# Plain fp32 products for batch 0's v and u, and a gate product in seven blocks for batches 1 to 7

## The chip, the cores and the metric

The program runs on one core of a Trainium2 chip. The metric is the time of one execution on the device, in microseconds (us). The core has TensorE (PE; its weight loads are PEld), VectorE (DVE), ScalarE (ACT), GpSimd (POOL) and SyncE (SP), which issues all DMAs here. Every engine works its own instructions off in order and waits for others by semaphores.

## The reference, cut to what matters

Eight batches. An attention over 8 heads, 576 positions and 64 columns (a pooled one over groups of 4 positions plus a local one over a band of 7) gives x; a gated MLP follows.

```
x = attention(q, k, v)                 # per batch 576 x 512
h = gelu(x @ w_in)                     # 512 -> 1024
u, v = h[..., :512], h[..., 512:]
v_n = (v - mean(v)) / sqrt(var(v) + 1e-6) * g_ln
v_s = einsum('ts,bsd->btd', w_sg, v_n) + b_sg[None, :, None]   # the gate product, 576 x 576
out = x + (u * v_s) @ w_out
```

## The kernel before, in words

Everything is kept turned: x, u and the gated product lie with the 512 columns on partitions (4 blocks of 128) and the 576 positions along the row, v with positions on partitions (4 blocks of 128 and one of 64).

`attention(b, p)` makes one pair of heads, 32 pairs in all, numbered g. It loads q, k and v (`lq`, `lk`, `lv`, `lw`), sums q, k and v over groups of four (`qs`, `ks`, `vs`), multiplies scores (`S`, the local ones, and `Y`, the pooled ones; from pair 4 on `YS` for both), takes maxima, exponentials and sums (`mx`, `my`, `ia`, `ib`, `ea`, `eb`, `ec`, `re`, `rc`), divides (`np`, `nq`), turns the probabilities on TensorE (`T`, `U`, `t`), copies them out of PSUM (`pa` to `pe`), multiplies with v (`D`) and writes x (`oe`, `od`, `xa`, `xb`). Then x is split into a high part in the rounded fp32 form that TensorE takes in one pass, and the rest (`xh`, `xl`, `xc`). These attention products are plain fp32 matmuls of 64 x 64 pieces, four of which run beside each other in the array.

`mlp(b)` makes three large products out of such splits; each is high x high, low x high and high x low: `v` (five blocks of 512 columns, in batch 0 in four steps each, `vk` and `v`), `u` (eight blocks of 288 columns), `s` (the gate product, eight blocks) and `o` (the output product). v goes through gelu (`vg`), mean and variance (`vb`), the root (`vp`), normalising (`vn`) and a split (`vh`, `vl`); u through gelu (`ua`); `sa` multiplies s by g_ln and adds b_sg on DVE, `sm` multiplies that with u. In batches 1 to 7 the output product is already made of seven block products per half instead of eight (`small_tasks`): sums of the gated blocks (`ga` to `gd`), their splits (`gh`, `gl`), products with combined weights (`zs`, `zh`, `zl`) and adds out of PSUM into x (`oa`). The result is stored by `os`.

The weights come as 64 bit words, are made fp32 by `wu`, `wq`, `wb` and `wt` and split by `wh` and `wl` (w_in as y0 to y3 for v and z0 to z3 for u, w_out as r0 to r3). The gate weights are fp32 and are split by `whq` and `wlq`.

What sets the order of the work is one list written out by hand, `ORDER`: each entry names a task and, behind a slash, its engine (without one, the first that the task names). `place` walks through it, gives each task its buffers (8 PSUM banks, 10 and 38 SBUF buffers) and the instructions are issued in that order, so every engine meets its share in it. A `dma` also waits for the sixth one before it. Ahead of `S0` stand 28 and ahead of `S3` 20 warming matmuls of zeros.

Lines that the rows below name: L244 is the copy helper, L481 `qs` and `ks`, L498 and L499 the two sums of `vs` on POOL, L514 and L535 the matmuls of `S` and `Y`, L613 `nq`, L693 part of `D`, L801 the matmuls of `v`, L896 those of `u`, `s` and batch 0's `o`, L887 `vl`, L943 `sa`, L924 `ua`, L1019 the seven block products of `o`, L1026 `oa`. L574, L596 and L817 are exponentials and gelus.

## Time and profile before

| | us |
|---|---|
| time, median of 3 runs (565.48 to 566.45) | 566.14 |
| the profiled execution, first to last instruction (its span) | 563.4 |
| PE busy | 547.7 (97%) |
| DVE busy | 445.5 (79%) |
| ACT busy | 392.7 (70%) |
| POOL busy | 331.9 (59%) |

For the profiled execution only its span is given; the time of the runs also holds what lies around the span, 2.7 us by the median. Busy time is the union of an engine's instructions. Matmuls overlap each other, so a mean of 295 ns for one does not say how far apart two start; the chain of work, which lists stretches of one line with their number, does. "<-" in a row of groups stands between what is written and what is read, and behind the bar stand the busy time, the mean ns of one, and the idle time of the engine just before them with what ended it. A window row has the length, then for each engine the busy us and in brackets its instructions, then the granted clock of TensorE, the share of the DMA engines and GB/s.

### The profile page before, as it was taken

Reading aid. Unit: us, or ns where it says so; the run is one execution under the profiler, and the core shown is the slowest. Engines: PE = TensorE matmul, PEld = TensorE weight load, DVE = VectorE, ACT = ScalarE, POOL = GpSimd, SP = SyncE. Lnnn points to the kernel's source line nnn. Section 1 sums busy time; section 2 is a strip of 40 time slices with the busy share of each in tenths; the row PEclk is TensorE's granted clock in tenths of the full one; section 3 lists DMA queues with packets and bytes.
Section 4 is the critical chain, followed back from the end, with each engine's and each line's share of the span. In section 5 each row is a group of like instructions: output and inputs, shape, how many; then the busy total and the mean of one; then the engine's idle time right before and its main releaser. Section 6 shows DMA issues by size and latency. Waiting matters only on the chain.

```text
span 563.4 us, 17546 instructions
## 1 busy us (share of the span) xinstructions
PE 547.7 (97%) x6948; PEld 511.2 (91%) x6948; DVE 445.5 (79%) x939; ACT 392.7 (70%) x1320; POOL 331.9 (59%) x447
## 2 busy tenths in 40 slices
PE   6888999999999999999999999999999999999997
PEld 4777899889998899989999899988999899999997
DVE  7998899977798887897869777886668786656565
ACT  2898899899876699177976976657956894525221
POOL 6895975856557665537764574528454573556222
PEclk8899999999999999999999999999999999999999
DMA  8879635310643144303441162403233224200004
GB/s 283 273 227 341 203 93 172 95 57 23 181 126 103 34 163 121 100 2 107 153 157 46 46 186 85 136 1 103 92 109 119 66 78 129 71 1 1 0 1 169
DMA packets 31041, 62.73 MB, mean 111 GB/s; under 512 B 3696, under 2 KB 4720, under 8 KB 30960
## 3 DMA queue, kind: packets, MB, share of 16 engines
q1 hardware_dynamic: 30960, 61.62, 34.3%
q8 instruction: 55, 0.90, 0.7%
q14 instruction: 26, 0.21, 0.1%
HBM read 52.17 MB, written 9.44 MB: 109 GB/s over the span
## 4 chain that ended last, share of the span: by engine, by line
PE 76%; ACT 6%; DVE 5%; POOL 4%; issue 2%; DMA 0%; DVEq 0%; ACTq 0%; POOLq 0%
PE ps L896 36%; PE ps L801 14%; PE ps L1019 12%; PE ps L677 3%; PE ps L693 2%; PE ps L616 2%; PE ps L625 2%; PE ps L535 2%; PE ps L514 2%; ACT X L574 2%; ACT R L244 1%; DVE R L990 1%; POOL pairs L498 1%; ACT pd L596 1%; POOL wsg_l L441 0%
## 5 line engine op out<-in xcount | busy, mean ns | idle before, releaser
L896 PE MATMUL ps<-wsg_h,R 128*128 128x288 f32 x576 | 122.5, 300 | 0.2 <-DVE R L887 0.2
L896 PE MATMUL ps<-X,weight_z 128*128 128x288 f32 x512 | 109.5, 297 | 0.3 <-ACT R L924 0.3
L801 PE MATMUL ps<-weight_y,X 128*128 128x512 f32 x320 | 98.3, 400 | 0.1
L574 ACT ACTIVATE X<-X,nb 128x64 f32<-128x64 f32 x280 | 93.5, 339 | 5.1 <-DVE nb L553 4.7
L896 PEld LDWEIGHTS ps<-wsg_h,R 128*128 128x128 f32 x576 | 93.9, 188 | 1.3 <-DVE R L887 0.4
L896 PE MATMUL ps<-wsg_l,R 128*128 128x288 f32 x320 | 92.6, 295 | 0.0
L896 PEld LDWEIGHTS ps<-X,weight_z 128*128 128x128 f32 x512 | 84.2, 188 | 1.2 <-ACT R L924 0.6
L896 PE MATMUL ps<-R,weight_z 128*128 128x288 f32 x256 | 75.4, 295 | 0.0
L801 PEld LDWEIGHTS ps<-weight_y,X 128*128 128x128 f32 x320 | 57.6, 188 | 11.9 <-POOL X L244 0.3
L1026 DVE TENSOR_TENSOR R<-ps,R 128x288 f32<-128x288 f32 x98 | 42.1, 448 | 25.2 <-PE ps L1019 24.9
L896 PEld LDWEIGHTS ps<-wsg_l,R 128*128 128x128 f32 x320 | 60.3, 189 | 0.0
L244 ACT COPY R<-ps 128x116 f32<-128x116 f32 (+3 forms) x80 | 27.2, 381 | 40.9 <-DVE R L244 11.9
L574 ACT ACTIVATION_READ_ACCUMULATOR X<-X,nb 128x1 f32 x280 | 53.3, 190 | 0.0
L1019 PE MATMUL ps<-R,weight_r 128*128 128x288 f32 x336 | 51.0, 298 | 0.3 <-DVE R L700 0.3
L244 ACT CAST R<-R 128x576 fp32r<-128x576 f32 (+2 forms) x61 | 39.1, 647 | 17.4 <-POOL R L990 10.5
L801 PE MATMUL ps<-weight_y,R 128*128 128x512 f32 x128 | 50.4, 394 | 0.0
L498 POOL TENSOR_TENSOR pairs<-R 112x256 f32<-112x256 f32 x56 | 45.0, 804 | 6.1 <-DMA R<-in_v_dram 6.0
L896 PEld LDWEIGHTS ps<-R,weight_z 128*128 128x128 f32 x256 | 48.2, 188 | 0.3
L943 DVE SCALAR_TENSOR_TENSOR vs<-ps,g_sb,b_sb 128x288 f32<-128x288 f32 x64 | 32.3, 512 | 20.1 <-PE ps L896 16.9
L1019 PEld LDWEIGHTS ps<-R,weight_r 128*128 128x128 f32 x336 | 46.6, 188 | 1.4 <-issue 0.5
L1002 POOL TENSOR_TENSOR R<-R,R 128x576 fp32r<-128x576 f32 x21 | 32.1, 1534 | 23.4 <-ACT R L244 9.8
L949 POOL TENSOR_TENSOR R<-R,vs 128x288 f32<-128x288 f32 x27 | 24.5, 909 | 35.4 <-DVE vs L943 29.4
(148 smaller groups left out, 1363.7 us busy)
## 6 DMA issues: line engine op xcount, KB each, us to landing
R<-in_v_dram SPq DMA_DIRECT2D x56, 224.0 KB, 3.5
X<-in_vw_dram SPq DMA_DIRECT2D x32, 320.0 KB, 4.4
R<-in_kT_dram SPq DMA_DIRECT2D x32, 293.0 KB, 3.9
R<-in_qT_dram SPq DMA_DIRECT2D x32, 293.0 KB, 3.8
out_dram<-R SPq DMA_DIRECT2D x28, 288.0 KB, 3.5
weight_z<-in_w_in_dram SPq DMA_DIRECT2D x4, 512.0 KB, 5.8
weight_y<-in_w_in_dram SPq DMA_DIRECT2D x4, 512.0 KB, 6.0
weight_r<-in_w_out_dram SPq DMA_DIRECT2D x4, 512.0 KB, 5.8
```

What stands on the lines that cost most here:

```text
L244: (nc.scalar.copy if e == "A" else ENG[e].tensor_copy)(**kw)
L498: ENG[e].tensor_tensor(out=pairs, in0=v[:, 0:2], in1=v[:, 2:4], op=ALU.add)
L514: nc.tensor.matmul(out=sp[i][os, c * KB:(c + 1) * KB], lhsT=q[hs, t * QB:t * QB + KB], rhs=k[hs, t * QB:t * QB + KB], start=not early, sto ...
L574: nc.scalar.activation(out=st["ms"][:, t, :], in_=src, func=AF.Exp, bias=st["nb"][:, t:t + 1], scale=scale, accum_out=sums[par][:, t:t + 1])
L677: nc.tensor.matmul(out=out, lhsT=lhsT, rhs=pdt[ks, probs, h * QC:(h + 1) * QC], start=first, stop=last)
L801: nc.tensor.matmul(out=acc, lhsT=r32(l), rhs=r32(weights[f"y{k}"][:, 0, w]), start=(i == 0 and ks[0] == 0), stop=(i == len(ops) - 1 and ks ...
L896: nc.tensor.matmul(out=acc[:, 0:HALF], lhsT=r32(l), rhs=r32(r), start=(first and n == 0), stop=(last and n == len(ops) - 1))
L943: nc.vector.scalar_tensor_tensor(out=vsb[i], in0=at["ps", "m", b, "s", i][:, 0:HALF], scalar=g_sb[:, i // 2:i // 2 + 1], in1=b_sb[:, half( ...
L949: ENG[e].tensor_tensor(out=gate(i), in0=gate(i), in1=vsb[i], op=ALU.mult)
L1002: ENG[e].tensor_tensor(out=r32(gl[m]), in0=us[raws[m]], in1=gh[m], op=ALU.subtract)
L1019: nc.tensor.matmul(out=bank(j, c), lhsT=r32(l), rhs=r32(r), start=first and i == 0, stop=i == len(ops) - 1, skip_group_check=not first)
L1026: nc.vector.tensor_tensor(out=x, in0=bank(j, c), in1=x, op=ALU.add)
```

## The change

Batch 0's v and u are made of plain fp32 matmuls with the whole weights and the whole x: 20 and 32 of them instead of 56 and 96, no split of x in batch 0, and the splits of w_in are first read by batch 1.

In batches 1 to 7 the first 512 of the 576 positions of the gate product are cut into two halves each way and made of seven block products per half of the columns and positions instead of eight: sums of normalised v blocks (`fa`, `fb`, `fd`, in place `fc`), their splits (`fh`, `fl`), combined gate weights made once (`ta`, `th`, `tl`), seven products for each of two column blocks, copies out of PSUM scaled by g_ln (`sx`) and joins (`sy`), and the gating (`sa`). The remaining 64 positions are added to four of the seven. The bias enters through these 64 positions' free rows, as b_sg / g_ln (`gr`, `gt`, `gs`, `br`, `bd`, `bs`, `be`; `vc` keeps a copy of the last block of v). The combined weights are written over parts of the old ones, after batch 0's last `s`.

`vs` can also run on DVE, as a reduction. The list `ORDER` is new throughout: other places, other engines. The diff, cut:

```diff
@@ ORDER @@
-wz3 wuz3 lk0 ks0/P wqz3/V wbz3 wy0 wqy0/V wby0 lq0 lk2 lk1 wtz3 whz3/A wlz3/P S0 lq1 qs0/V Y0 mx0 ia0 lq3 my0 ks1/P
-wuy0 qs1/P ib0 ea0 small wty0 S1 mx1 ks2/V lq2 qs2/P ia1 es0 ny0/A ec0 re0/A ib1 ea1 Y1 lk3 my1 rc0 S2 mx2 why0/A ia2
...
+lk0 ks0 lq0 S0 qs0 Y0 mx0 wz3 wqz3 lq1 wy0 my0 lk1 lk2 wbz3 ia0 ib0 qs1/P ks1/P ny0 wqy0 lq2 qs2/P ks2/P ea0 wby0 ec0
+wuz3 S1 mx1 lq3 es0 re0 lk3 Y1 my1 ny1 ec1 lv0 S2 mx2 ks3/P S3 rc0 np0 ia1 ib1 ea1 wuy0 wz0 ia2 ib2 T0 ea2 nq0 lq4 es1
...
@@ SMALL_S, and what is prepared once @@
-EARLY_S, EARLY_D, WIDE, SMALL_O = 4, 4, 4, 1
+EARLY_S, EARLY_D, WIDE, SMALL_O, SMALL_S = 4, 4, 4, 1, 1
...
+    def guard(out, g):
+        nc.vector.tensor_scalar(out=out, in0=g, scalar1=TINY, scalar2=2.0 * TINY, op0=ALU.is_lt, op1=ALU.mult)
+        nc.vector.scalar_tensor_tensor(out=out, in0=g, scalar=-TINY, in1=out, op0=ALU.is_gt, op1=ALU.mult)
+        nc.vector.tensor_tensor(out=g, in0=g, in1=out, op=ALU.add)
...
+    def g_turn(e):
+        raw, tmp = at["R", "w", "g"][up, 0:DM], buf("R", "w", "g2")[up, 0:DM]
+        guard(tmp, raw)
+        nc.vector.reciprocal(out=raw, in_=raw)
...
+    def b_rows_of(dst, raw):
+        nc.vector.tensor_copy(out=r32(dst), in_=raw)
+        nc.vector.tensor_tensor(out=raw, in0=raw, in1=dst, op=ALU.subtract)
+        nc.vector.tensor_scalar(out=r32(dst), in0=dst, scalar1=row_sb[up, 1:2], scalar2=None, op0=ALU.mult)
+        nc.vector.scalar_tensor_tensor(out=r32(dst), in0=raw, scalar=row_sb[up, 0:1], in1=dst, op0=ALU.mult, op1=ALU.add)
...
+    def t_sum(n):
+        def emit(e):
+            buf("R", "tr", n)
+            for i in range(2):
+                a, c = {1: lambda: (t_raw(i, False), t_raw(i, True)), 2: lambda: (t_raw(2 + i, False), t_part(1, i)),
+                        3: lambda: (t_raw(2 + i, False), t_raw(i, False)), 4: lambda: (t_raw(2 + i, True), t_part(2, i))}[n]()
+                ENG[e].tensor_tensor(out=t_part(n, i), in0=a, in1=c, op=ALU.subtract)
+        return emit
...
+    for n, raws, before in ((1, (0, 1), []), (2, (2, 3), ["ta1"]), (3, (0, 1, 2, 3), []), (4, (2, 3), ["ta2"])):
+        add(f"ta{n}", {"P": 1.5, "V": 0.8}, t_sum(n), [f"tq{i}" for i in raws] + before, takes=[("R", "tr", n)],
+            gives=[("R", "tq", i) for i in raws] + [("R", "tr", n - 1)] * len(before))
+        add(f"th{n}", {"A": 0.58, "V": 0.4}, t_high(n), [f"ta{n}"] + ([f"s{SMALL_S - 1}.{i}" for i in range(2 * KT)] if n == 1 else [f"sm{SMALL_S - 1}.{i}" for i in range(2 * KT)] if n == 3 else []))
+        add(f"tl{n}", {"P": 1.3, "V": 0.66}, t_low(n), [f"th{n}"], gives=[("R", "tr", n)])
@@ attention @@
+                if e == "V":
+                    nc.vector.tensor_reduce(out=vd[:, i], in_=v.rearrange("p f d -> p d f"), axis=AX.X, op=ALU.add)
+                    continue
-            add(N("vs"), {"P": 2.7}, vsum, [N("lv"), N("D", 2)], gives=[("R", "v4", g, 0), ("R", "v4", g, 1)])
+            add(N("vs"), {"P": 2.7, "V": 1.3}, vsum, [N("lv"), N("D", 2)], gives=[("R", "v4", g, 0), ("R", "v4", g, 1)])
+        if b == 0:
+            return
         add(N("xh"), {"A": 0.64, "V": 0.4}, x_high, [N("xa"), N("xb")], takes=[("X", "xh", g)])
@@ mlp: v and u of batch 0 @@
+                if first:
+                    for k in ks:
+                        l = sb[k]["x"][:, s * P:min(S, (s + 1) * P)]
+                        nc.tensor.matmul(out=acc[0:LEFT] if last else acc, lhsT=l, rhs=unsplit(f"y{k}"), start=k == 0, stop=k == KT - 1)
+                    return
...
+                if first:
+                    acc = buf("ps", "m", b, "u", i)[:, 0:HALF]
+                    for k in range(KT):
+                        l = block(unsplit(f"z{k // 2 * 2 + d}"))[:, k % 2, ds]
+                        nc.tensor.matmul(out=acc, lhsT=l, rhs=sb[k]["x"][:, cs], start=k == 0, stop=k == KT - 1)
+                    return
...
@@ mlp: the seven block products of batches 1 to 7 @@
+        def f_sum(n):
+            def emit(e):
+                buf("R", "f", b, n)
+                for i in range(2):
+                    near, far = vact[i][0], vact[2 + i][0]
+                    a, c, op = {1: lambda: (near[:, DM // 2:], far[:, DM // 2:], ALU.add),
+                                2: lambda: (f_tile(1)[:, i], near[:, 0:DM // 2], ALU.subtract),
+                                4: lambda: (far[:, 0:DM // 2], f_tile(2)[:, i], ALU.subtract)}[n]()
+                    ENG[e].tensor_tensor(out=f_tile(n)[:, i], in0=a, in1=c, op=op)
...
+        def f_self(i):
+            def emit(e):
+                v = vact[i][0]
+                ENG[e].tensor_tensor(out=v[:, DM // 2:], in0=v[:, 0:DM // 2], in1=v[:, DM // 2:], op=ALU.subtract)
...
+        def s_mm_s(j, n):
+            c, first_in = {1: "b", 2: "a", 5: "e"}.get(n) or {3: "e"}.get(n, "b"), n in (1, 2, 5)
+
+            def emit(e):
+                if first_in:
+                    buf("ps", "m", b, "s", j, c)
+                ops = []
+                for i in range(2):
+                    ops += [(s_left(n, i, x, j), s_right(n, i, y)) for x, y in ((0, 0), (1, 0), (0, 1))]
+                if n in (2, 3, 4, 7):
+                    ds = slice((j + (2 if n in (4, 7) else 0)) * P, (j + (3 if n in (4, 7) else 1)) * P)
+                    cs = slice(0, HALF) if n == 2 else slice(HALF, S)
+                    for l, c0 in ((vhat[NS - 1][0], 0), (last_sb, 1)):
+                        ops.append((l[:, ds], wsd[c0] if n == 4 else (wsg_h, wsg_l)[c0][:, NS - 1, cs]))
+                for i, (l, r) in enumerate(ops):
+                    nc.tensor.matmul(out=s_bank(j, c), lhsT=r32(l), rhs=r32(r), start=first_in and i == 0,
+                                     stop=i == len(ops) - 1, skip_group_check=not first_in)
+            return emit
...
+                    buf("R", "t", b, j, k // 2)
+                src, g = s_bank(j, "bbe"[k]), g_sb[:, d:d + 1]
+                if e == "A":
+                    nc.scalar.activation(out=s_part(j, k), in_=src, func=AF.Copy, scale=g)
+                else:
...
+            def emit(e):
+                nc.vector.scalar_tensor_tensor(out=s_part(j, k), in0=s_bank(j, "aeb"[k]), scalar=g_sb[:, d:d + 1], in1=s_part(j, k),
+                                               op0=ALU.mult, op1=ALU.add)
+            return emit
...
+            def emit(e):
+                if (r, t) == (1, 0):
+                    nc.vector.scalar_tensor_tensor(out=gate(i), in0=s_bank(j, "b"), scalar=g_sb[:, d:d + 1], in1=gate(i),
+                                                   op0=ALU.mult, op1=ALU.mult)
+                else:
+                    ENG[e].tensor_tensor(out=gate(i), in0=gate(i), in1=s_part(j, r + t), op=ALU.mult)
+            return emit
...
+        if small_s:
+            for n, need, used in ((1, [N("vn", i) for i in range(4)], (0, 1, 2, 3)), (2, [f"fa{b}"], (0, 1)), (4, [f"fb{b}"], (2, 3))):
+                gives = [("R", "v", b, i) for i in used] + ([("R", "f", b, {2: 1, 4: 2}[n])] if n > 1 else [])
+                add(f"f{'abcd'[n - 1]}{b}", {"P": 1.5, "V": 0.7}, f_sum(n), need, takes=[("R", "f", b, n)], gives=gives)
+                add(N("fh", n), {"A": 0.58, "V": 0.4}, f_high(n), [f"f{'abcd'[n - 1]}{b}"], takes=[("R", "fh", b, n)])
+                add(N("fl", n), {"P": 1.3, "V": 0.66}, f_low(n), [N("fh", n)], takes=[("R", "fl", b, n)], gives=[("R", "f", b, n)])
+            for i in range(2):
+                add(N("fc", i), {"P": 0.75, "V": 0.35}, f_self(i), [f"fa{b}"])
         for s in range(NS):
...
+            fac = {1: ["vl", 0, 1], 2: ["vl", 2, 3], 3: ["fl", 4], 4: ["vl", 2, 3], 5: ["fl", 1], 6: ["fl", 2], 7: ["vl", 0, 1]}
...
+                prod(1, "b", opens_bank=True)
+                add(X_(0), copied, s_copy(j, 0), [S_(1)] + (["sg"] if b == SMALL_S else []), takes=[t0])
+                prod(2, "a", opens_bank=True)
+                add(Y_(0), joined, s_join(j, 0), [S_(2), X_(0)], gives=[key("a")])
+                prod(6, "b", [X_(0)])
+                add(X_(1), copied, s_copy(j, 1), [S_(6), X_(0)])
+                prod(5, "e", opens_bank=True)
+                add(X_(2), copied, s_copy(j, 2), [S_(5)], takes=[t1])
+                prod(3, "e", [X_(2)])
+                add(Y_(1), joined, s_join(j, 1), [S_(3), X_(1)], gives=[key("e")])
+                prod(7, "b", [X_(1)])
+                add(Y_(2), joined, s_join(j, 2), [S_(7), X_(2)])
+                prod(4, "b", [Y_(2)])
+                for r, t, need, gives in ((0, 0, Y_(0), [t0]), (0, 1, Y_(1), [t0]), (1, 1, Y_(2), [t1]), (1, 0, S_(4), [key("b")])):
+                    i = 2 * (j + 2 * r) + t
+                    add(N("sa", i), {"V": 0.51} if gives[0][0] == "ps" else {"P": 0.83, "V": 0.46}, s_gate_s(i), [need, N("ua", i)], gives=gives)
         if small_o:
             small_tasks()
             return
...
```

## Rows read from the trace of the kernel before

**Rows 1.** The page's first part: busy time of each engine.
```profile
PE 547.7 (97%) x6948; PEld 511.2 (91%) x6948; DVE 445.5 (79%) x939; ACT 392.7 (70%) x1320; POOL 331.9 (59%) x447
```

**Rows 2.** Windows: stretch, length, PE, PEld, DVE, ACT, POOL busy, clock, DMA, GB/s.
```profile
0.00:60.00 60.00, 49.02 (x985) 40.34 (x989) 51.48 (x120) 43.76 (x146) 45.31 (x59) 0.94 0.87 279
60.00:88.00 28.00, 27.72 (x423) 25.80 (x414) 25.84 (x59) 26.39 (x83) 20.55 (x31) 1.00 0.47 160
88.00:173.20 85.20, 85.18 (x1178) 80.64 (x1176) 71.27 (x145) 74.30 (x263) 55.73 (x72) 1.00 0.32 96
173.20:540.00 366.80, 365.57 (x4234) 344.40 (x4228) 281.15 (x588) 244.52 (x822) 204.59 (x283) 1.00 0.27 84
```

**Rows 3.** Waits of TensorE, whole span: line, releaser, total us, times, longest.
```profile
PE ps L514 <- DMA R<-in_qT_dram: 2.3, 1, 2.3
PE ps L693 <- issue: 2.2, 1, 2.2
PE ps L535 <- DVE qd L481: 2.1, 2, 1.4
PE ps L625 <- POOL pd L613: 1.7, 1, 1.7
...
PE ps L535 <- ACT R L244: 0.7, 1, 0.7
```

**Rows 4.** The chain of waits: start us, us, what and how many.
```profile
114.26 2.78 PE ps L801 x12
126.22 12.73 PE ps L896 x96
...
547.55 12.70 PE ps L1019 x96
560.27 0.46 DVE R L1026
```

**Rows 5.** Groups by shape, TensorE: split products, then the pooled scores.
```profile
L896 PE MATMUL ps<-wsg_l,R 128*128 128x288 f32 x320 | 92.6, 295 | 0.0
...
L801 PE MATMUL ps<-weight_y,R 128*128 128x512 f32 x128 | 50.4, 394 | 0.0
...
L535 PE MATMUL ps<-kd,qd 64*64 64x144 f32 x256 | 16.5, 303 | 2.9 <-DVE qd L481 2.1 <-ACT R L244 0.7
...
L535 PE MATMUL ps<-kd,qd 64*64 64x48 f32 x128 | 11.1, 221 | 0.4 <-issue 0.4
```

**Rows 6.** Groups: weight loads of the gate product.
```profile
L896 PEld LDWEIGHTS ps<-wsg_l,R 128*128 128x128 f32 x320 | 60.3, 189 | 0.0
```

**Rows 7.** Groups: operations of DVE and POOL that the new ones resemble.
```profile
L498 POOL TENSOR_TENSOR pairs<-R 112x256 f32<-112x256 f32 x56 | 45.0, 804 | 6.1 <-DMA R<-in_v_dram 6.0
L1026 DVE TENSOR_TENSOR R<-ps,R 128x288 f32<-128x288 f32 x98 | 42.1, 448 | 25.2 <-PE ps L1019 24.9
L943 DVE SCALAR_TENSOR_TENSOR vs<-ps,g_sb,b_sb 128x288 f32<-128x288 f32 x64 | 32.3, 512 | 20.1 <-PE ps L896 16.9 <-issue 2.3 <-POOL R L949 0.5
L499 POOL TENSOR_TENSOR vd<-pairs 112x128 f32<-112x128 f32 x56 | 28.8, 514 | 4.4
L887 POOL TENSOR_TENSOR R<-R,R 128x512 fp32r<-128x512 f32 (+1 forms) x17 | 22.0, 1299 | 16.5 <-ACT R L244 5.4 <-DVE R L244 5.1 <-ACT R L924 4.1
L887 DVE TENSOR_TENSOR R<-R,R 128x512 fp32r<-128x512 f32 (+1 forms) x23 | 17.5, 767 | 4.2 <-ACT R L244 2.1 <-POOL rs L854 1.8
L481 DVE TENSOR_REDUCE qd<-R 128x144 f32<-128x576 f32 x23 | 17.1, 742 | 1.0 <-DMA R<-in_qT_dram 1.0
```

**Rows 8.** Groups: ACT's table loads, the first and the last of six lines.
```profile
L924 ACT ACT_TABLE_LOAD x13 | 16.7, 1283 | 0.4
...
L362 ACT ACT_TABLE_LOAD x1 | 1.3, 1283 | 0.7 <-PEq L1210 0.7
```

**Rows 9.** Groups: the seven block products of the output.
```profile
L1019 PE MATMUL ps<-R,weight_r 128*128 128x288 f32 x336 | 51.0, 298 | 0.3 <-DVE R L700 0.3
...
L1019 PE MATMUL ps<-R,R 128*128 128x288 f32 x252 | 39.2, 299 | 0.6 <-DVE R L1026 0.6
```

More of the change, by code (lines that the diff above doesn't have):

```diff
@@ L293 @@
     nm3 = [const.tile([P, 1], F32, name=f"nm{i}") for i in range(3)]
-    vs2 = [const.tile([P, HALF], F32, name=f"vs{i}") for i in range(2)]
+    vs_both = buffers.tile([P, S], F32, name="wst3l")
+    vs2 = [vs_both[:, 0:HALF], vs_both[:, HALF:S]]
     nc.vector.memset(zeros, 0.0)
@@ L310 @@
     nc.vector.memset(nhalf, -0.5)
+    nc.vector.tensor_copy(out=row_sb[:, 0:1], in_=ident_sb[:, KB + 1:KB + 2])
+    nc.vector.tensor_scalar(out=row_sb[:, 1:2], in0=row_sb[:, 0:1], scalar1=-1.0, scalar2=1.0, op0=ALU.mult, op1=ALU.add)
     for t in qd2 + od2:
@@ L323, with b_diff @@
+    def b_diff(e):
+        raw, dif = at["R", "w", "b"][up], buf("R", "w", "bd")[up, 0:HALF]
+        ENG[e].tensor_tensor(out=dif, in0=raw[:, 0:HALF], in1=raw[:, HALF:S], op=ALU.subtract)
     add("small", {"S": 0.5}, lambda e: dma("S", out=g_sb, in_=small), mb=0.01)
     add("b", {"S": 0.5}, lambda e: dma("S", out=b_sb, in_=b_sg.broadcast_to([P, S])), mb=0.3)
+    add("sg", {"V": 0.3}, lambda e: guard(g_tmp, g_sb), ["small"])
+    add("gr", {"S": 0.5}, g_load, takes=[("R", "w", "g")], mb=0.13)
@@ new lines @@
+    add("gt", {"V": 2.6}, g_turn, ["gr"], takes=[("R", "w", "g2")], gives=[("R", "w", "g2")])
+    add("gs", {"V": 0.8, "P": 1.6}, g_split, ["gt"], gives=[("R", "w", "g")])
+    add("br", {"S": 0.5}, b_load, takes=[("R", "w", "b")], mb=0.15)
+    add("bd", {"V": 0.4, "P": 0.8}, b_diff, ["br"], takes=[("R", "w", "bd")], gives=[("R", "w", "b")])
+    add("bs", {"V": 2.2}, lambda e: b_rows_of(wsg_l[up, NS - 1, :], at["R", "w", "b"][up, 0:S]), ["bd"] + [f"s{SMALL_S - 1}.{i}" for i in range(2 * KT)], gives=[("R", "w", "b")])
@@ L329 @@
+    add("be", {"V": 1.4}, lambda e: b_rows_of(wsd[1][up], at["R", "w", "bd"][up, 0:HALF]), ["bd"], gives=[("R", "w", "bd")])
     weights = {}
@@ new lines @@
+    for s in range(NS):
+        add(f"tq{s}", {"S": 0.5}, t_load(s), takes=[("R", "tq", s)], mb=0.3)
+    for n, raws, before in ((1, (0, 1), []), (2, (2, 3), ["ta1"]), (3, (0, 1, 2, 3), []), (4, (2, 3), ["ta2"])):
[3 more added lines that the diff above has]
+        add(f"tl{n}", {"P": 1.3, "V": 0.66}, t_low(n), [f"th{n}"], gives=[("R", "tr", n)])
@@ new lines, in d_raw, with d_sum, d_high, d_low @@
+    def d_raw():
+        return at["R", "tq", 4][:, 0:HALF]
+    def d_sum(e):
+        ENG[e].tensor_tensor(out=d_raw(), in0=d_raw(), in1=at["R", "tq", 4][:, HALF:S], op=ALU.subtract)
+    def d_high(e):
+        copy(e, out=r32(wsd[0]), in_=d_raw())
+    def d_low(e):
+        ENG[e].tensor_tensor(out=r32(wsd[1][0:KB]), in0=d_raw()[0:KB], in1=wsd[0][0:KB], op=ALU.subtract)
+    add("ta5", {"P": 0.8, "V": 0.4}, d_sum, ["tq4"])
+    add("th5", {"A": 0.38, "V": 0.3}, d_high, ["ta5"])
+    add("tl5", {"P": 0.8, "V": 0.4}, d_low, ["th5"], gives=[("R", "tq", 4)])
@@ L812, in emit @@
                 vact[s] = [v]
-                if s == NS - 1:
+                if s == NS - 1 and first:
+                    total = dict(accum_out=sum5[s][0:LEFT]) if by_scalar(s) else {}
+                    nc.scalar.activation(out=v[0:LEFT], in_=acc[0:LEFT], func=AF.Gelu_apprx_tanh, **total)
+                elif s == NS - 1:
                     copy(e, out=v[0:LEFT], in_=acc[LEFT:P])
@@ L945, in s_bias, with s_names @@
             return emit
+        def s_names(n):
+            return [f"s{n}.{j}{m}" for j in range(2) for m in (2, 3, 4, 7)] if n >= SMALL_S else [f"s{n}.{i}" for i in range(2 * KT)]
         def s_gate(i):
@@ L1085, in mlp @@
             c = 1.9 if last else 2.8
-            w = [f"wly{i}" for i in range(KT)] if first else []
+            w = [f"{'wty' if first else 'wly'}{i}" for i in range(KT)] if b < 2 else []
             if first:
@@ L1096, in mlp @@
                     gives=xs)
-            if last:
+            if last and not first:
                 add(N("va", s), {"A": 0.58, "V": 0.6}, v_act(s), [N("v", s)], takes=[("R", "v", b, s)])
@@ L1115, in mlp @@
                 gives=[("ps", "m", b, "u", i)], func="g")
-        for i in range(2 * KT):
+        for i in range(0 if small_s else 2 * KT):
             w = [f"wlq{s}" for s in range(NS)] + ["b", "small"] if first else []
```

368 lines of the change are left out of this document (239 added, 129 removed).

## The prediction

> **What bounds the kernel now.** The page's first part comes first: TensorE is busy for 547.7 of the 563.4 us, DVE for 79% [rows 1]. The windows then show where it is not: in the first 60 us it works 49.0 us, from 60 to 540 us it lacks 1.5 us in all [rows 2]. Between 60 and 88 us DVE is at 92% and ACT at 94%, and TensorE still gets 99% [rows 2], so two full helpers did not stop it there. TensorE's waits say the same: those for the attention's data, 2.3 for the DMA of q, 2.2 unexplained, 2.1 for DVE's pooled q, 1.7 for POOL's probabilities and 0.7 for ACT, together 9.0 us, all lie in the first 60 us [rows 3]. At the other end TensorE runs without a gap to 560.25 us, and one add and its store make the last 3.2 us [rows 4]. So there are two places to gain: TensorE's own work, and its first 60 us. The danger is a helper that no longer keeps up.
>
> Everything is summed against the 563.4 us of the span; the median of the runs, 566.14, is 2.7 us above it, and I keep that distance.
>
> **Products that go.** A gate product of a batch is 8 outputs of 14 matmuls, 112. As seven blocks per half it is 2 x (3 x 6 + 4 x 8) = 100. An unbroken run of 96 matmuls of this shape took 12.73 us, 132.6 ns each [rows 4]; 12 x 7 x 0.1326 = **11.1 us less**.
>
> **Products that become plain fp32.** Batch 0 has v in 56 matmuls of 512 columns, 232 ns each (12 in 2.78 us [rows 4]), 13.0 us, and u in 96 of 288, 12.7 us. After it they are 20 and 32, but a plain one stands twice in the trace: the pooled scores issue 8 per pair of heads, 256 in all, and have 512 records (256 and 128 of the shapes shown, 128 of one between them) [rows 5]. No row has a full-sized plain product, so I take the slope over columns: 303 ns at 144 and 221 at 48 are 0.85 ns per column, against (394 - 295)/(512 - 288) = 0.44 for the split products [rows 5]. The split ones have some 5 ns beside the slope from start to start, so a pass takes 443 ns at 512 and 251 at 288: 40 x 0.443 + 64 x 0.251 = 33.8 us, **8.1 us more**. Bounds: were a pass as quick as a split matmul, 40 x 0.232 + 64 x 0.1326 = 17.8 us (7.9 less than now); if each of the 104 weight loads, 189 ns [rows 6], stood bare in front of its pass, 19.7 us more again. The slope is measured on the same kind of instruction, so I keep 8.1. Nothing hides this: it is TensorE's own time. Products together: **-3.0 us**.
>
> **The first 60 us.** Batch 0 needs no xh, xl and xc any more and only the whole weights, and the order is new. Three things shorten the way.
> S0 waits 2.3 us for q [rows 3], as the order issues two weight blocks and the first k ahead of it, 1.65 MB with q; now it is the first k and q alone, 0.6 MB, at the 279 GB/s of this stretch [rows 2] 2 us instead of 6, and both land while the 28 warming matmuls run. That gives back 2.3. Then ks0 and qs0 run on DVE while S0 runs, so the wait for pooled q loses its larger piece, 1.4. Of the other 5.3 I count 1.5: from the start to v0.0 the order's entries times the mean durations of their lines make 40 us of DVE instead of 50, 33 of POOL instead of 47, and 12.3 MB of DMA instead of 14.2, but the chain of the first pairs (maximum, exponential, reciprocal, turn) stays. **-5.2 us**, between 0 and all 9.0.
>
> **What DVE, ACT and POOL get.** Per batch: three sums, each two operations of 256 columns, about as many elements as one L887 operation, 0.77 us on DVE or 1.30 on POOL; their three high and three low parts at the same price; two in-place differences; six scaled copies out of PSUM (0.45, L1026's price on DVE); the eight 0.51 us operations of L943 stay eight, and eight gatings become six [rows 7]. Once, around batch 1: four combinations of the gate weights with their splits and the bias and 1/g rows, 15.3 us if DVE does it all. In exchange the order moves other work: 22 of the 28 vs go from POOL (two pairs of 0.80 + 0.51 us, 2.64 [rows 7]) to a DVE reduction. I priced every entry of both orders with the mean of its line: DVE 493 to 515 us, POOL 333 to 364, ACT 437 to 471. The same tally overshoots the old DVE, 445.5 [rows 1], by 10% (records overlap), so DVE comes to 465 us, 83% of the span. ACT gets something back: exponentials and gelus alternate 48 times in the old order, which is the number of table loads (six lines, x13 down to x1, 1.283 us each [rows 8]), and 40 times in the new one, 10.3 us less.
>
> That the block form can be fed at all is in the trace: the output product of batches 1 to 7 is already made of seven blocks, with its sums and joins, and its 588 matmuls saw 0.9 us of idle time [rows 9].
>
> The stretch to fear lies between the first s of batch 0 and the first v of batch 2. Before, 83.9 us of TensorE's work there took 85.2 us, with 71.3 of DVE [rows 2] and 79.7 in my tally, a factor of 0.894. In the new order this stretch has 92.4 us of TensorE's work and, setup included, 98.6 of DVE in the tally, 88.1 after the factor: 95%, where it was 84%. Inside it, over 46 us from v1.4 to the first v of batch 2, DVE's entries exceed TensorE's work by 10 us; the largest such excess after the start is 6 in the old order, and cost under 0.7 us. Not all can be done ahead, since the new weights wait for batch 0's last s (they are written over the old). I take **+3 us**, between 0 (60 to 88 us shows that 92% costs nothing) and 6 (what exceeds the excess of before, plus 2 of latency).
> Behind it DVE's load from v of batch 2 to s of batch 7 rises from 79% to 84% of TensorE's work: **+1**, bounds 0 and 4. At the end two products of batch 6 no longer stand between the products of batch 7, and gd7, gl7.1 (0.9 each) and a gating (0.5) follow the last s against 2.4 us of three products: **+0.4**, 0 to 1. The stores are as before.
>
> **A reduction across lines.** The vs on DVE reads its four addends 512 bytes apart. No DVE row reads so; the nearest is L481, 0.74 us for 576 addends side by side [rows 7], which gives 2 x 0.66 = 1.32 per vs and is what the tally holds. At worst it is as slow as POOL's pair, 2.64. [...]
>
> **Sum.** -3.0 - 5.2 + 3 + 1 + 0.4 = -3.8: a span of 559.6, a time of **562.3 us**; its own range 558 to 565. Chance 50%.
>
> **Rivals.**
> 1. *The start gives all and DVE keeps up.* The 9.0 us go and the batch 1 stretch costs 1: -3.0 - 9.0 + 1 = 555. For it: DVE, POOL and DMA all have less before v0.0. Against: the chain of the first pairs is as long as it was, and 2.2 us are unexplained. 13%.
> 2. *DVE takes the start's gain back.* If 95% of DVE means DVE sets the pace of the batch 1 stretch, being early at its beginning is worth nothing at its end: only -3.0 and a few tenths elsewhere, less 2 to 3 of later stalls: 565.5. For it: the excess of 10 us. Against: 60 to 88 us. 13%.
> 3. *Slower: the DVE vs costs 2.6 us and not 1.3.* 22 x 1.32 = 29 us more DVE. Three 25 us stretches (about batches 3 to 5) stand at 92 to 94% by the tally; with four or five such vs in each pair of stretches they pass 100%. At 5% loss over these 75 us, 4 us, with 2.6 in batch 1: 562.3 + 6.6 = 569. It decides from about 1.8 us per vs, where these stretches reach 97%. For it: addends 512 bytes apart. Against: the reduction has one SBUF input and reads without a partner. 15%.
> 4. *Bare weight loads of the plain passes*: 562.3 + 19.7 = 582. Against: loads of 189 ns lie wholly beside split matmuls that start every 133 ns [rows 4, 6], and a plain pass is longer. 4%.
> 5. *The plain products are not twice as dear per pass*: 5.8 to 15.9 us less, 554 at the likelier end, were the slope one of small tiles only. 5%.
>
> **Numbers.** About 0.2% (1.1 us) is what can be told from no change: 565.0 to 567.3. Faster: most of the forecast (48), rival 1 (13), rival 5 (5), a little of rival 2 (2): 68%. Same: 10%, nearly all of it rival 2. Slower: 22%: rival 3, rival 4 and the upper tails. The range 555 to 571 leaves out rival 4, half of rival 5, the lower half of rival 1 and the upper part of rival 3, under 20%.
>
> **What would show it.** L1019's and v's records unchanged in batches 1 to 7, gate products 12 matmuls fewer per batch at 133 ns; batch 0's u and v passes at 0.25 and 0.44 us from start to start, with no gap for weights; TensorE busy some 54 us of the first 60; S0's first matmul near 6.2 us instead of 8.5; 40 table loads; DVE near 95% before v of batch 2 and TensorE's only later waits there, on DVE; the reductions of vs at 0.66 us each. It is wrong if TensorE's waits after 60 us exceed 6 us, if a plain pass is over 0.5 us at 512 columns, or if the first 60 us lose as much as before.

## The result, and the profile after

The kernel after takes 569.92 us (median of 4 runs, 567.57 to 575.09) where the one before takes 565.81 beside it (4 runs, 565.04 to 566.45): ratio 1.0105, 95% interval 1.0065 to 1.0146. It is **slower**; the forecast was 562.3 and faster. The profiled run is the quickest of the four, 567.57 us with a span of 565.7, so the profiles differ by 2.3 us and the medians by 4.1; what follows accounts for the 2.3 of the profiled run.

First the page's engine row of the kernel after, which answers to [rows 1], then its windows, the stretches and columns of [rows 2].
```profile
PE 545.8 (96%) x6816; PEld 496.3 (88%) x6816; DVE 481.0 (85%) x993; ACT 412.6 (73%) x1390; POOL 369.1 (65%) x440
```
```profile
0.00:60.00 60.00, 51.95 (x1006) 36.91 (x1007) 48.33 (x122) 41.61 (x146) 42.34 (x57) 1.00 0.85 272
60.00:88.00 28.00, 28.00 (x329) 20.74 (x328) 27.55 (x56) 26.15 (x78) 21.82 (x23) 1.00 0.55 170
88.00:173.20 85.20, 80.48 (x1026) 75.91 (x1026) 78.60 (x156) 67.02 (x247) 60.52 (x67) 0.96 0.34 107
173.20:540.00 366.80, 363.16 (x4295) 340.72 (x4293) 309.18 (x628) 272.96 (x912) 235.57 (x289) 1.00 0.28 89
```
The first row is the page's; each of the four others is one window. TensorE is busy for 2.9 us more of the first 60 and 4.7 less of the third stretch, where its clock fell to 0.96 of full. DVE, 445.5 us before, has 481.0. TensorE's longest waits over the span (columns of [rows 3]):
```profile
PE ps L743 <- POOL pd L731: 3.9, 2, 3.6
PE ps L811 <- issue: 2.8, 1, 2.8
PE ps L653 <- ACT pd L714: 1.6, 1, 1.6
```
The waits behind the first 60 us add up to 8.3 us, more than the 6 that the prediction named as a sign of being wrong. The first row is new at this place. It is in the main one wait of 3.6 us near 150 us, in front of pair 10's turned probabilities. What led to it stands in the chain (start us, us, what), which is DVE's for 20 us:
```profile
127.44 0.44 DVE R L339
127.90 0.70 DVE R L340
128.62 0.70 DVE R L341
129.35 0.30 DVE R L349
129.65 0.09 issue
129.76 2.95 issue
...
147.61 1.18 POOL R L1036
148.79 2.66 POOL pd L731
151.50 0.62 PE ps L743 x2
...
153.69 2.89 PE ps L1127 x12
...
159.51 1.60 PE ps L1127 x12
```
L339 to L349 make the row of 1/g for batches 1 to 7, on 64 partitions of 512 elements. The 2.95 us of "issue" behind L349 are the rest of its one instruction, which runs from 129.35 to 132.70 us. L1036 and L731 are POOL's last two steps before the turn. The last two rows are the clock: 12 products take 2.89 us after the wait, 241 ns each, and 1.60 us six us later, 133 each. Two groups of DVE say why it was late (columns of [rows 7]):
```profile
L613 DVE TENSOR_REDUCE vd<-R 112x128 f32<-112x512 f32 x44 | 45.7, 1080 | 0.0
L349 DVE RECIPROCAL R<-R 64x512 f32<-64x512 f32 x1 | 3.3, 3349 | 0.0
```
L613 is the vs reduction, priced at 660 ns; L349 is the reciprocal. The prediction has no price for it alone. The list of tasks in the kernel has 2.6 us for all four operations of L339 to L349, and the other three take 1.8 of them, so some 0.8 us were left for it.

**Where the time went.** I call TensorE's lateness at a task its start in the profile less the TensorE work written ahead of it (each matmul at its own interval from start to start). Its growth between two tasks is what the stretch between them lost, to waits or to a low clock. In us, for all kernels of this study (the tasks: batch 0's first joint product of v; pair 7's output, behind five of batch 0's eight gate blocks; batch 2's first v; batch 7's first v; the end):
```
               v of b0  pair 7  v of b2  v of b7   end
before           20.5    22.2    23.4     29.4    32.4
after            15.9    16.8    25.5     35.4    38.9
e1_vs_side       19.7    20.2    27.6     36.0    39.5
e2_recip_early   25.7    26.6    28.4     37.5    40.7
e3_both          25.4    25.9    27.1     34.5    37.7
e4_warm          18.2    19.0    25.3     36.3    39.8  (3.2 of it the added matmuls)
e6_no_recip      19.4    20.3    23.6     33.4    36.9
e7_narrow        17.8    24.9    28.4     38.0    41.6
e8_narrow_side   18.1    21.6    26.0     33.9    37.4
e9_few_side      18.5    19.0    22.6     30.0    33.4
e10_few          18.6    21.2    25.4     34.5    38.0
e11_start        16.8    17.2    20.8     28.7    32.0
```
TensorE's own work went from 531.0 to 526.8 us, -4.2. Lateness to pair 7: -5.4. From pair 7 to v of batch 2: 8.7 instead of 1.2, +7.5. On to v of batch 7: 9.9 instead of 6.0, +3.9. Behind it: +0.5. Together +2.3, the difference of the spans.

### The profile page after: what moved, and what is told of

Read it like the earlier page. It is cut to its first block, busy times and chain, and to the rows that moved or that the text cites. A ratio compares the mean times of both kernels' runs of the same rounds, so it can differ in the third digit from the quotient of the medians.

```text
span 565.7 us, 17437 instructions
## 1 busy us (share of the span) xinstructions
PE 545.8 (96%) x6816; PEld 496.3 (88%) x6816; DVE 481.0 (85%) x993; ACT 412.6 (73%) x1390; POOL 369.1 (65%) x440
## 3 DMA queue, kind: packets, MB, share of 16 engines
q1 hardware_dynamic: 31840, 63.37, 35.3%
## 4 chain that ended last, share of the span: by engine, by line
PE 74%; DVE 15%; ACT 5%; issue 3%; POOL 2%; DMA 1%; DVEq 0%; ACTq 0%; POOLq 0%
PE ps L926 15%; PE ps L1081 14%; PE ps L1127 13%; PE ps L1262 13%; PE ps L795 3%; PE ps L734 3%; PE ps L632 3%; PE ps L811 3%; PE ps L743 2%; DVE vd L613 2%; PE ps L653 2%; PE ps L1454 1%; PE ps L919 1%; ACT X L692 1%; DVE R L818 1%
## 5 line engine op out<-in xcount | busy, mean ns | idle before, releaser
L1127 PE MATMUL ps<-X,weight_z 128*128 128x288 f32 x448 | 96.6, 299 | 0.9 <-DVE R L1221 0.9
L926 PE MATMUL ps<-weight_y,X 128*128 128x512 f32 x280 | 84.7, 396 | 0.0
L728 POOL TENSOR_TENSOR X<-X,rc 128x640 f32<-128x640 f32 x26 | 37.9, 1458 | 35.4 <-DVE rc L725 30.5
L1081 PE MATMUL ps<-wsg_h,R 128*128 128x288 f32 x266 | 58.4, 300 | 0.2 <-POOL R L1016 0.2
L1269 DVE TENSOR_TENSOR R<-ps,R 128x288 f32<-128x288 f32 x98 | 42.3, 450 | 15.9 <-PE ps L1262 15.5
L1016 POOL TENSOR_TENSOR R<-R,R 128x512 fp32r<-128x512 f32 (+1 forms) x22 | 30.9, 1406 | 34.7 <-ACT R L248 9.4
L248 ACT COPY R<-ps 112x192 f32<-112x192 f32 (+4 forms) x87 | 31.0, 397 | 21.3 <-PE ps L734 8.7
L613 DVE TENSOR_REDUCE vd<-R 112x128 f32<-112x512 f32 x44 | 45.7, 1080 | 0.0
L1081 PEld LDWEIGHTS ps<-wsg_h,R 128*128 128x128 f32 x266 | 43.8, 188 | 0.6 <-POOL R L1016 0.4
L1161 ACT ACTIVATE R<-ps 128x288 f32<-128x288 f32 x64 | 24.5, 410 | 20.5 <-PE ps L1127 18.4
L714 ACT ACTIVATE pd<-ps,nbd 128x144 f32<-128x144 f32 x96 | 35.2, 376 | 4.4 <-DVE nbd L683 3.9
```

The costliest lines, as they stand in the source:

```text
L248: (nc.scalar.copy if e == "A" else ENG[e].tensor_copy)(**kw)
L613: nc.vector.tensor_reduce(out=vd[:, i], in_=v.rearrange("p f d -> p d f"), axis=AX.X, op=ALU.add)
L714: nc.scalar.activation(out=pd[:, n], in_=st["sdv"][n].rearrange("p (c k) -> p c k", c=3), func=AF.Exp, bias=st["nbd"][:, n:n + 1], scale=s ...
L728: ENG[e].tensor_tensor(out=st["ms"], in0=st["ms"], in1=bc_last(st["rc"][:, 0:NT], KB), op=ALU.mult)
L926: nc.tensor.matmul(out=acc, lhsT=r32(l), rhs=r32(weights[f"y{k}"][:, 0, w]), start=(i == 0 and ks[0] == 0), stop=(i == len(ops) - 1 and ks ...
L1016: ENG[e].tensor_tensor(out=r32(dst), in0=vact[s][0][0:n], in1=vh[0:n, 0:DM], op=ALU.subtract)
```

## Experiments

The theory: DVE has more to do than priced, by the strided vs all along and by the 1/g row in the batch 1 stretch, and the wait there lowers the clock besides. Each kernel was timed beside the kernel before, whose medians there were 565.2 us (e1 to e4), 565.5 (e5 to e8), 564.5 (e9, e10) and 564.3 (e11). The ratio is to that, and is not the quotient of the two medians; where that matters, both sizes are given. Each lateness and each wait comes from one profiled execution of a kernel.

**e1_vs_side**: from batch 1 on, the four addends of a value sum lie side by side.
```diff
-            ... .rearrange("p (f d) -> p f d", f=FAC)
+            ... .rearrange("p (f d) -> p f d" if early_d else "p (d f) -> p d f", f=FAC)
-    nc.vector.tensor_reduce(out=vd[:, i], in_=v.rearrange("p f d -> p d f"), axis=AX.X, op=ALU.add)
+    nc.vector.tensor_reduce(out=vd[:, i], in_=v, axis=AX.X, op=ALU.add)
```


> The changed kernel, with v for batches 1 to 7 laid out so that the four addends of a pooled value lie side by side: the DVE reduction of vs reads lines instead of steps of 512 bytes; nothing else moves. Theory (DVE is overfull, and these reductions are part of it): a reduction falls from 1.08 to about 0.66 us, DVE's busy time from 481 to 462, the loss behind batch 1 (4.5 us more than before between D10 and the v of batch 7) shrinks by 2 to 4 us, the wait in batch 1 hardly moves: 565 to 567. Rival (the order and POOL set the waits, DVE's price does not matter): reductions cheaper, time 569 to 570.

567.87 us, 1.0034 (1.0006 to 1.0061), DVE 467.5 us. The reduction, on the same elements, now costs what was forecast:
```profile
L613 DVE TENSOR_REDUCE vd<-R 112x128 f32<-112x512 f32 x44 | 27.9, 674 | 0.0
```
The kernel is 2 us faster than the kernel after by the medians, 4 by the ratios, and still waits 3.6 us at pair 10: the stride is one cost of two. The time lies just above the 565 to 567 of the theory, and the loss from v of batch 2 to v of batch 7 shrinks by 1.5 us, less than the 2 to 4 expected.

**e2_recip_early**, **e3_both**: the kernel after, and e1, with the 1/g row made first of all.
```diff
-lk0 ks0 lq0 S0 qs0 ...  gr ...  gt ...  gs ...
+gr gt gs lk0 ks0 lq0 S0 qs0 ...
```


> The changed kernel with the load, reciprocal and split of the 1/g row (gr, gt, gs: 5.2 + 2.1 us on DVE, 3.35 of it one reciprocal of 512 columns) at the head of the order, where DVE waits for the first k. Theory (DVE's work piled up between 124 and 150 us makes the wait of 3.6 us before t10): that wait and the clock lost by it go, 4 to 6 us less: 564 to 566, with at most 1 us more at the start. Rival (POOL's nq10, held back by its own queue, sets the wait): 569 to 570, same wait.

> Both edits. Theory: they add up, DVE 462 us busy, 7 to 9 us less than the changed kernel: 561 to 563, and faster than the kernel before. Rival: not under 567.

568.58 us, 1.0035 (1.0002 to 1.0068), and 566.18, 1.0013 (0.9978 to 1.0047); 564 to 566 and 561 to 563 were expected. The stretch from pair 7 to v of batch 2 costs 1.8 and 1.2 us instead of 8.7: the loss there is gone. But the start pays: TensorE waits 5.3 and 4.0 us for DVE's first pooled q, which stands behind the reciprocal, and is 25.7 and 25.4 us late at v of batch 0. Most of the time moved, it did not go. The wait of e2:
```profile
PE ps L653 <- DVE qd L596: 5.3, 1, 5.3
```

**e4_warm**: 30 matmuls on zeros in front of pair 10's turn, as the kernel already has at two places.
```diff
-WARM = {"S0": 28, "S3": 20}
+WARM = {"S0": 28, "S3": 20, "t10": 30}
```


> The changed kernel with 30 more warming matmuls of zeros (109 ns each, 3.3 us) in front of t10, where TensorE waits 3.6 us. The wait for t10 stays, so nothing is lost by them, and TensorE is not idle. If the lost clock behind this wait (half speed for some us in the window 88 to 173 us, mean 0.96) is part of the loss, 1.5 to 2 us less, 566 to 568, and the runs lie closer together; if the clock costs nothing, 569 to 570.

569.08 us, 1.0061 (1.0033 to 1.009). The wait falls to 0.6 us, the clock of the third stretch is 1.00, and the stretch loses 6.3 us with the 3.2 of the added work in it, instead of 8.7. So the low clock cost some 2.4 us in it; in the time, with 11.0 us lost behind it and 2.3 more at the start, it does not show: 566 to 568 were expected.

**e5_before_q_first**: the kernel before, with the first k and q loaded first.
```diff
-wz3 wuz3 lk0 ks0/P wqz3/V wbz3 wy0 wqy0/V wby0 lq0 lk2 ...
+lk0 lq0 wz3 wuz3 ks0/P wqz3/V wbz3 wy0 wqy0/V wby0 lk2 ...
```


> The kernel before with one thing of the change: the loads of k and q of the first head pair stand first in the written order, ahead of the two 512 KB weights. Theory (the change's gain in the first 60 us, 5.4 us of TensorE's lateness, comes from these two loads): TensorE's first real product comes about 2.3 us earlier (near 6.2 instead of 8.5 us), and the kernel is about 2 us shorter, some 563.5 against 565.5, ratio 0.996. Rival (the gain comes from the rest of the new order; the weights that now land later delay their splits by as much): no change within 0.2%, ratio 0.998 to 1.002.

566.56 us, 1.0019 (1.0000 to 1.0038): the rival. The loads did what they should, and DVE gave it back (timeline of TensorE: start us, us, what, idle before it):
```profile
6.14 0.93 PE L513 MATMUL ps<-R,R 64*64 64x64 f32 x40
10.95 1.30 PE L534 MATMUL ps<-kd,qd 64*64 64x144 f32 x16 [3.88 <-DVE qd L480]
```
The first product comes at 6.14 us, and the second waits 3.9 us for the pooled q, since DVE's queue still has the weights' work in front of it. A load moved alone gains nothing; the change had moved DVE's work as well.

**e6_no_recip**: the reciprocal in place becomes a copy, so the division of 1/g is left out.
```diff
-        nc.vector.reciprocal(out=raw, in_=raw)
+        nc.vector.tensor_copy(out=raw, in_=raw)
```


> The kernel after with the reciprocal over the 512-element row of the gain replaced by a plain copy in place (so it leaves the reciprocal out): the instruction stays where it is in VectorE's queue, but takes about 0.4 us instead of 3.35. Theory (these 3 us, in a stretch where VectorE has no pause between 124 and 151 us, are what makes the copies of batch 1 late): TensorE's lateness grows by about 3 to 4 us less from pair 7 to pair 10 (7.3 to 8.0 with the reciprocal), the 3.6 us wait in front of pair 10's turned sums shrinks under 1.5 us, and the stretch from 88 to 173 us loses less at half clock; ratio to the kernel after about 0.993, that is 565 to 566 us against 569. Rival (the stall is the piled-up order as a whole, with POOL's 2.7 us product of pair 10's pooled weights last): the wait stays over 2.5 us and the time within 1 us of the kernel after.

565.25 us, 0.9988 (0.9957 to 1.0019). The stretch loses 3.3 us instead of 8.7, the wait at pair 10 is 1.8 (under 1.5 expected), and the clock stays full there.
```profile
PE ps L743 <- POOL pd L731: 1.8, 1, 1.8
```
One instruction of 3.35 us was worth 5.4 us of that stretch, its wait and the clock behind it included, and 4.7 of the time against the 569.92 of the kernel after (6.6 by the ratios). The rival, POOL's product last in line, holds for what is left of the wait: that product still takes 2.67 us, 1.8 over its median of 0.91.

**e7_narrow**, **e8_narrow_side**: the reciprocal on 128x4, through a line in device memory; e8 with e1's layout.
```diff
-        guard(tmp, raw)
-        nc.vector.reciprocal(out=raw, in_=raw)
+        nc.vector.reciprocal(out=g_tmp, in_=g_sb)
+        dma("S", out=g_line.rearrange("o (k p) -> p (o k)", p=P), in_=g_tmp)
+        dma("S", out=buf("R", "w", "g")[up, 0:DM], in_=g_line.broadcast_to([P - KB, DM]))
```


> The kernel after with the reciprocal taken on the 128x4 layout of the gain that the kernel holds anyway (once checked for zeros already, so that the second check goes as well), stored to a line of 2 KB in device memory and loaded from there to the 64 partitions: the same values, 4 elements per partition instead of 512, at the price of two DMAs. From the row of 13 elements (234 ns) the reciprocal is estimated at about 0.2 us, so VectorE has about 4.5 us less to do in the stretch (3.35 + 0.43 + 0.69 + 0.69 less 0.2, the latter some 60 us earlier). Theory: as for the plain copy or better, about 565 us, ratio to the kernel after 0.993 or less; the wait in front of pair 10 under 1 us. Rival: within 1 us of the kernel after.

> The narrow reciprocal and, for the values of batches 1 to 7, the layout in which the four addends lie side by side (0.67 us a reduction instead of 1.08). Theory (the two costs are separate and add up): the narrow reciprocal's time less a further 1.5 to 2 us, about 563 us, TensorE's lateness after batch 1 growing by about 8 to 9 us instead of 10.6; that is below the kernel before by some 2 us, ratio to before about 0.996. Rival (both costs are hidden by the same slack once one of them goes): no better than the narrow reciprocal alone.

569.78 us, 1.0059 (1.0026 to 1.0092), and 565.60, 0.9993 (0.9967 to 1.0019). The batch 1 stretch is cured (3.5 and 4.4 us; the wait at pair 10 is 1.9 in both, not under 1) and the layout is worth 4.2, but both miss their forecast by some 3 to 5 us, and the table says where: between v of batch 0 and pair 7 they lose 7.1 and 3.5 us, the kernel after 0.9. In e7 the chain shows a pause in the middle of one unbroken product:
```profile
87.83 4.58 PE ps L1131 x33
92.41 3.67 issue
96.08 3.97 PE ps L1131 x15
```
Behind it the clock is at half from 94.4 to 101.2 us, most of the rest of the 7.1. e8 has a pause of 2.7 us that ends at 90.3 us. The DMA view of 83 to 93 us of e7 shows 1.13 MB moved while the DMA engines are busy for 87%; this is e7, then e9, whose store is coarser:
```profile
DMA packets 1100, 1.13 MB, mean 113 GB/s; under 512 B 576, under 2 KB 576, under 8 KB 1100
```
```profile
DMA packets 1351, 2.64 MB, mean 264 GB/s; under 512 B 168, under 2 KB 168, under 8 KB 1350
```
My store was 512 pieces of 4 bytes, started at 83 us. One queue of the same DMA engines, q8, is for instructions and brings blocks of 16 KB (54 in e7's trace, 0.7% of the engines' time), taken here to be TensorE's code; the blocks that come at 87.0 and 90.8 us in the kernel after come at 93.7 and 99.1 in e7. That the fine store held the block up is argued from these times; the next pair tests it, together with two moved steps.

**e9_few_side**, **e10_few**: the reciprocal on 16x32, stored in pieces of 128 bytes; two steps moved; e9 with the side-by-side layout, e10 without.
```diff
-        dma("S", out=g_line.rearrange("o (k p) -> p (o k)", p=P), in_=g_tmp)
+        dma("S", out=g_line.rearrange("o (p j) -> (o p) j", p=16), in_=g_inv)
-... rc10 o0.6 np10 ... fb1/V nq10 th1 ...     ... pb27/V vs27/V my28 ma28 ... ny28/V lk30 ...
+... rc10 nq10/V o0.6 np10 ... fb1/V th1 ...   ... pb27/V my28 ma28 ... ny28/V vs27/V lk30 ...
```


> The narrow reciprocal and the side-by-side values again, with three edits. (a) The gain is loaded a second time as 16 rows of 32 elements and its reciprocal stored in 16 pieces of 128 bytes instead of 512 pieces of 4 bytes: the theory that those pieces held up TensorE's next block of code (it came at 93.7 us with the narrow reciprocal against 87.0 and 90.8 in the kernel after, and TensorE stood 3.7 us) says that the pauses put to issue between 85 and 100 us (3.7 and 2.7 us) go; the rival, that they are chance, says that one of 2 us or more is there again. (b) The product of pair 10's pooled weights goes from POOL (2.67 us, 1.9 us of TensorE's waiting) to VectorE right behind pair 10's reciprocal: that wait goes, and 1 to 2 us with it. (c) The value sums of pair 27 go behind the bound of pair 28's pooled scores: the wait of 1.1 us near 436 us shrinks. Sum: 4 us less than the narrow reciprocal with the values side by side (565.6), that is 561 to 562 us, ratio to before 0.993; the rival, that each wait is followed by another, gives 564 to 566.

> The same kernel with the values as in the kernel after (the four addends of a sum 512 bytes apart, 1.08 us a reduction instead of 0.67). VectorE has 42 x 0.41 = 17 us more to do. Theory (the strided sums cost the time only where VectorE is late): 2 to 4 us more than with the values side by side, ratio to before 0.997 to 1.000. Rival (no cost once the reciprocal is out of the way): the same time within 1 us.

e9: **561.89 us, 0.9953 (0.9925 to 0.9982)**, faster than before and after. e10: 566.45, 1.0021 (0.9994 to 1.0049). The pauses put to issue between 85 and 100 us are gone in both. So is the wait for POOL's product of pair 10's pooled weights, though 1.6 us of it come back as a wait of pair 10's output for a copy of ACT's. The wait near 436 us, 1.1 us in e8, is 0.4 in e9. The layout alone is worth 4.6 us (3.8 by the ratios), more than the 2 of e1 by the medians, though not more than its 4 by the ratios: 2.1 between v of batch 0 and pair 7, 0.6 in the batch 1 stretch, 1.7 behind it. The 2.1 are not all the layout's: the kernel after and e6 have the same layout and lose 0.9 there, and e10's trace has a wait of 1.2 us in front of 81.6 us, for a copy of ACT's, which theirs do not have. The 4.6 reject the rival of no cost, and sit slightly over the upper end expected.

**e11_start**: e9, with pair 1's k loaded before the second weight and six plain passes of v between the outputs of pairs 2 and 3.
```diff
-... wqz3 lq1 wy0 my0 lk1 lk2 ...   ... vk0.0 vk1.1 ... vk3.0 ... D2 ... D3 ...
+... wqz3 lq1 lk1 wy0 my0 lk2 ...   ... D2 vk0.0 vk1.1 vk3.0 ... D3 ...
```


> The kernel with 16 x 32 reciprocal, side-by-side values and the two order edits (561.9 us, ratio 0.9953), with two further edits of the written order, both in the first 60 us. (a) The load of pair 1's k goes from behind the second 512 KB weight to in front of it. (b) Of batch 0's v, three products by single pairs (six plain passes, 2.6 us of TensorE) go from in front of pair 2's output to between pair 2's and pair 3's. Theory: in the first 60 us TensorE's clock fell to half twice, after a wait for k of 2.0 us or more (near 11 us) and after the pause put to issue inside pair 3's output (2.2 to 3.1 us, near 46 us), and the kernel after was profiled in a run with neither fall; pair 2's and pair 3's outputs, 208 small matmuls in 5 us, use up TensorE's code faster than the next block of it comes. So (a) cuts the wait for k under 1 us, (b) cuts the pause under 1 us, the granted clock of the first 60 us is 0.99 or 1.00, TensorE is 2 to 4 us less late at the first joint product of v (16 us or less against 18.5), and the time is 558 to 560 us, ratio to before 0.990. Rival (the pause is not one of code used up, or another load is late in k's place): the time within 1 us of 561.9, the pause still over 2 us.

560.60 us, 0.9924 (0.9894 to 0.9955). The wait for k is 0.9 us and pair 3's pause is gone, but one of 1.7 us stands in pair 2's output, followed by half clock from 39.8 to 43.2 us. v of batch 0 is 1.7 us less late than in e9: less than expected, more than the rival allows. The time is 1.3 us under e9's, short of the 558 to 560 expected, and the intervals of the two ratios overlap. It is the fastest version of this study by its median.

## Why the prediction was wrong

- **Products, -3.0: right, -4.2 measured.** A plain pass starts every 429 ns at 512 columns and every 243 at 288: 40 x 0.429 + 64 x 0.243 = 32.7 us against 33.8 worked out. No weight load stands bare: the trace has 0.0 us of idle time before the plain passes of both shapes. The chain has 8 passes in 3.46 us (432 ns each), the timeline 16 short ones in 4.06 from the first one's start to the last one's end:
```profile
47.43 3.46 PE ps L919 x8
```
```profile
75.62 4.06 PE L1138 MATMUL ps<-R,R 128*128 128x288 f32 x16
```
- **The first 60 us, -5.2: right in the profiled run, -5.4, by luck, and too much in general.** It was profiled with the clock at 1.00 throughout, while the profile before has half clock from 11.1 to 14.6 and from 24.8 to 28.2 us. In the seven other kernels with this order up to v of batch 0 (e1, e4, e6 to e10) lateness there is 17.8 to 19.7 us, against 15.9 in the profile of the kernel after and 20.5 before: 0.8 to 2.7 us less late, not 5.2. The windows of the kernel after and of e6 in two places show what differs:
```profile
10.00:16.00 6.00, 4.71 (x114) 3.82 (x115) 5.93 (x14) 3.80 (x14) 4.37 (x8) 1.00 0.86 292
46.00:52.00 6.00, 5.97 (x29) 3.28 (x30) 4.27 (x9) 2.37 (x4) 3.32 (x4) 1.00 1.06 327
```
```profile
10.00:16.00 6.00, 4.97 (x105) 3.91 (x106) 5.13 (x13) 4.58 (x17) 4.31 (x8) 0.72 0.72 237
46.00:52.00 6.00, 5.29 (x22) 3.51 (x23) 4.27 (x9) 2.15 (x6) 3.44 (x5) 0.50 1.05 285
```
  e6 waited 2.6 us for pair 1's k before the first of these and 2.8 in pair 3's output before the second; the kernel after waited 1.1 and 2.8, and its clock did not fall: the same pause of 2.8 us came with a fall and without one. The four runs of the kernel after have mean clocks of 0.994, 0.988, 0.991 and 0.985 in the order 565.7, 569.7, 566.4 and 573.2 us of span. That the clock makes most of this spread is borne out by the kernel before: of its 31 executions beside e1 to e4, the four with a mean clock of 0.999 or 1.000 have spans of 560.3 to 561.0 us, the three with 0.988 or less 565.8 to 569.1. Where in the execution the clock fell is known only for the traced ones. TensorE was busy for 52 us of the 60, not 54, and its first product came near 7.5 us, not 6.2 (6.1 to 7.5 in the seven others).
- **The batch 1 stretch, +3 (0 to 6): the step that failed, +7.5.** The +3 rests on DVE at 95%: 88.1 us of its work on 92.4 of TensorE's. From the first s of batch 0 to the first v of batch 2 the kernel after takes 94.8 us, 8.7 of them lost (all behind pair 7's output), so TensorE's work is 86.1; e3 takes 87.2 for all of it, losses included. The two windows, of the kernel after and of e3:
```profile
85.86:180.61 94.75, 90.03 (x1197) 85.22 (x1192) 87.94 (x173) 75.72 (x285) 67.74 (x74) 0.96 0.37 114
```
```profile
94.98:182.22 87.24, 87.18 (x1198) 82.70 (x1193) 79.86 (x167) 75.50 (x285) 61.23 (x74) 1.00 0.40 122
```
  DVE's sum came out, 87.9 us, but it is 102% of TensorE's work and not 95%: DVE was no longer a helper with room, it set the pace. That was the condition of the second rival, and as in it the start's gain was gone at its end: TensorE is 25.5 us late at v of batch 2, against 23.4 before. The loss follows DVE's work in this stretch: 79.9 us of it lose 1.2 (e3), 80.9 lose 1.8 (e2), 84.8 lose 3.3 (e6), 86.9 lose 7.4 (e1), 87.9 lose 8.7 (after); e7 to e10, with 81.0 to 84.5, lose 3.5 to 4.4.
  What put DVE over the edge is the price of "the bias and 1/g rows" within "15.3 us if DVE does it all". The four operations up to the reciprocal took 5.2 us where the kernel's list has 2.6, and the row's split, a cast of 0.94 and a difference of 1.18 at 140.2 us, took 2.1 where it has 0.8; the sum came out all the same, so other entries were priced too high. The trace of before held the rows that should have warned, DVE's reciprocals of 13 elements beside its operations of one element:
```profile
L607 DVE RECIPROCAL rc<-sums 128x13 f32<-128x13 f32 x32 | 7.5, 234 | 4.4 <-ACT sums L601 4.3
L844 DVE TENSOR_SCALAR rs<-mv 128x1 f32<-128x1 f32 x11 | 1.7, 154 | 0.5
```
  That is some 7 ns per element. The reciprocals of this study (178 ns at 4, 341 at 32, 3349 at 512 elements of a partition) cost 6.3 ns per element between 32 and 512. The 3.35 us are 7.9 times the 0.43 of the operation with one input of the same size (L339); no run here shows what makes a reciprocal so long. Without the long reciprocal the stretch costs 3.3 to 4.4 us (e6 to e10), 2.1 to 3.2 over before: the +3 is what the setup costs without it. And the prediction had no term for the clock: TensorE was at half speed from 150.2 to 157.0 us.
- **Behind it, +1 (0 to 4): +3.9.** With the strided reduction this stretch loses 9.1 to 11.0 us (after, e2, e4, e6, e7, e10), with the side-by-side one 7.4 to 8.4 (e1, e3, e8, e9, e11), before 6.0. The four pairs that differ in the layout alone give the stride 1.5 to 1.7 of it. The other 1.4 to 2.4 belong to the rest of the change, likely to denser work on all helpers; no run separates it further.
- **The third rival was half of the truth.** A vs costs 2 x 1.08 = 2.16 us, past the 1.8 from which it was to decide. It was to cost 6.6 us and cost 4.6 (e9 against e10). Its 569 us lie next to the 569.92 measured partly by luck: it did not hold the 1/g row, which came on top. The traces show what the stride costs, 1.08 us (after) against 0.67 side by side (e1) for the same 512 addends, but not by what mechanism.
- **The fifth rival's price can't be redone.** Its least gain of 5.8 us and its 554 follow from no row shown, and the passes came out at 32.7 us, near the full price.
- **Tail +0.4: +0.5. Table loads 40: right.** Five lines, 12 and 12 to 1:
```profile
L1161 ACT ACT_TABLE_LOAD x12 | 15.4, 1283 | 0.2
...
L401 ACT ACT_TABLE_LOAD x1 | 1.3, 1283 | 0.7 <-PEq L1506 0.7
```
- **DVE in all, 465 forecast: 481.0.** 44 reductions x (1.08 - 0.66) = 18.5 us and 2.7 of the reciprocal are more than the whole excess; e9, without both, has 463.8. POOL was forecast at 364 and has 369.1.
